# A down projection cut into 512 and 128 columns, its leftovers gathered in one PSUM bank, and every step of the kernel in a new order

## Chip, cores and metric

The kernel runs on one core of a Trainium2 chip. The metric is device time in microseconds (us), lower is better; a run is compared with runs of the other kernel on the same chip. One execution of each kernel is also profiled, and its trace is what this document reads.

## What is computed

Two branches work on the same layer-normed input and are added to it. The input A_q has S = 2048 rows and D = 640 columns; the gated unit has an inner width of F = 1728. All operands are bf16.

```python
x  = A_q
xn = layernorm(x)                                    # over the 640 columns, no gain
# branch A: a convolution over the 2048 rows, channel by channel
k_shift = sum over t of k[s-t] * shift_k[:, t]       # 4 taps
kv = k_shift * v
y  = causal convolution of kv with ssm_k (length 2048, by FFT of length 4096) + kv * ssm_D
A  = xn * y
# branch B: a gated unit
h  = sigmoid(xn @ w_gate) * (xn @ w_up)              # 2048 x 1728
B  = h @ w_down                                      # 2048 x 640
return x + A + B
```

The input `B_x` is not used.

## The kernel before

**Layout.** Row s of the input sits on partition s // 16, in block s % 16, so that a tile of 128 partitions by 16 blocks by 640 columns (`x`, and `xn` for its normed copy) holds everything. The sum builds up in `x`: each branch adds its part there, and the stores read it.

**Branch B** runs in four row groups t of four blocks each. For a group, `xn` is transposed into `xnT` (by TensorE for t = 0, by DMA transposes, `xn_turn`, for the others). Then for each of 13 chunks fc of 128 inner columns, `gate_mm` and `up_mm` (line 291) each make five matmuls of 128x512 into a PSUM tile. ScalarE (ACT) takes the sigmoid (`gate_ev`, line 300), and VectorE (DVE) multiplies it with the up product into `hT` (`up_ev`, line 306). The last 64 inner columns of both go through one product (`both_mm`, line 312; `both_ev`, line 318; `both_mul`, line 321). The down projection follows: for each block bb of the group, 14 matmuls over fc with a 128x128 block of `hT` as the stationary operand and `wd` as the moving one. Before the change it does this once for columns 0 to 319 and once for columns 320 to 639, except for the very last block, which is cut at 512. Each half is issued as two steps of seven matmuls (`down_mm`, line 335), and DVE adds the PSUM result onto `x` (`down_ev`, line 340).

**Branch A** runs in five chunks c of 128 channels, as an FFT convolution in two stages each way:

- `kv_op` (DVE, lines 368 to 377, 16 per chunk) makes kv; `h_turn` (DVE, line 354) transposes the kernel's taps.
- `st1_mm` (lines 393 and 395, 8 per chunk) is the first stage; `st1_ev` copies its PSUM out into tiles `t1`, of which there are two; `wr1` writes each filled tile to DRAM.
- `rd2` reads it back in another layout into tiles `t2`, of which there are two; `st2_mm` (line 427, 4 groups per chunk, numbered s = 0 to 19) is the second stage; `st2_ev` copies it into one of three slots of `xz` (slot s mod 3).
- `prod` multiplies the spectra on DVE: part 0 is a shuffle (line 440), part 1 a multiply (line 442).
- `inv1_mm` (line 456, two per chunk, numbered y = 0 to 9, each on two slots) is the first inverse stage; `inv1_ev` copies out; `wr2` writes to DRAM; `rdb` reads back into `bi`.
- `inv2_mm` (line 495, 4 per chunk) ends the transform; `inv2_q` (line 500) multiplies with `xn` and `inv2_x` (line 505) adds onto `x`.

The PSUM copies of `st1_ev`, `st2_ev` and `inv1_ev` go to ACT (line 254) or to DVE (line 257). PSUM is two pools: `psC`, two tiles of two banks, for branch A's stages (`st2_mm` and `inv1_mm` fill both tiles at once), and `psG`, four tiles of one bank, for all products, down parts and `inv2_mm`.

**Order.** The two branches share all engines. Nothing is scheduled by a planner at build time: steps are appended to chains, one letter a kind (`g` products and down parts, `a` st1_mm, `b` st2_mm, `c` inv1_mm, `d` inv2_mm, `k` kv_op, `u` DVE's steps of branch B, `m` the first loads, `o` the stores, and so on), and a string `ORDER` of one letter a step says in which order they are issued. A capital F, J or I in it is a copy that goes to DVE instead of ACT. `TURNS` reorders the loads and stores within their chains. Each engine then runs its own steps in that order and waits by semaphores. SyncE (SP) issues nearly all DMAs, in the same order; a wait there holds up every later DMA.

Of the kernel before, what the change touches and what calls it, by code (L numbers as in the profile page):

```python
# [11 lines left out]
F32 = mybir.dt.float32  # L12
U16 = mybir.dt.uint16
ACT = mybir.ActivationFunctionType
ALU = mybir.AluOpType

S = 2048
DM = 640
FF = 1728
P = 128  # L20
NB = S // P
NC = DM // P
NFC = 14
# [42 lines left out]
def kernel(  # L66
# [14 lines left out]
    nc = tc.nc  # L81
# [19 lines left out]
    psG = ctx.enter_context(tc.tile_pool(name="psG", bufs=4, space=bass.MemoryType.PSUM))  # L101
# [14 lines left out]
    x = res.tile([P, NB, DM], BF16, name="x")  # L116
# [4 lines left out]
    wd = res.tile([P, NFC, DM], BF16, name="wd")  # L121
    hT = res.tile([P, NFC, 512], BF16, name="hT")
# [199 lines left out]

    pds = {}

    def cols(t, bb, half):
        m = 4 * P if (t, bb) == (3, 3) else DM // 2
        return slice(m, DM) if half else slice(0, m)

    def down_mm(t, bb, half, part):
        es = cols(t, bb, half)  # L330
        if part == 0:
            pds[bb, half] = psG.tile([P, es.stop - es.start], F32, name="pd", tag="g")
        pd = pds[bb, half]
        for fc in range(7 * part, 7 * part + 7):
            nc.tensor.matmul(pd[:, :], lhsT=hT[:, fc, bb * P:(bb + 1) * P], rhs=wd[:, fc, es],  # L335
                             start=(fc == 0), stop=(fc == NFC - 1))

    def down_ev(t, bb, half):
        es = cols(t, bb, half)
        nc.vector.tensor_tensor(x[:, 4 * t + bb, es], pds[bb, half][:, :], x[:, 4 * t + bb, es], ALU.add)  # L340

    def store(b0, b1, lo, hi):
        (nc.scalar if b1 == NB and hi == DM else sync).dma_start(outr[:, b0:b1, lo:hi], x[:, b0:b1, lo:hi])
# [218 lines left out]
    def step(k, fn, *args):  # L562
        chains[k].append((fn, args))

    for t in range(4):
        for fc in range(0 if t else 2, 13):
            step("g", gate_mm, t, fc)
            step("s", gate_ev, t, fc)
            step("g", up_mm, t, fc)
            step("u", up_ev, t, fc)  # L570
        step("g", both_mm, t)
        step("s", both_ev, t)
        step("u", both_mul, t)
        firsts = [(0, 0, 0), (0, 1, 0), (0, 0, 1), (0, 1, 1)]
        for bb, e, part in firsts + [(k // 2, k % 2, n) for k in range(2, 8) for n in range(2)]:
            step("g", down_mm, t, bb, e, part)
            if part:
                step("u", down_ev, t, bb, e)

    def hs(c):  # L580
        return [(load_h, c)]
# [77 lines left out]
        for i in range(4):  # L659
            step("e", xn_turn, g, i)  # L660

    for b in range(0, 12, 2):
        step("o", store, b, b + 2, 0, 4 * P)
    for b in (0, 4, 8):
        step("o", store, b, b + 4, 4 * P, DM)
    for b in range(12, NB - 1):
        step("o", store, b, b + 1, 0, DM)
    step("o", store, NB - 1, NB, 0, 4 * P)
    step("o", store, NB - 1, NB, 4 * P, DM)

    ORDER = """
    mgmLggmmmssugmLuggsmZgmusmmgggmgmuLkHHLgsuksmkggsgmmmuusPlllmmggguklTkkkskkmugsgkumkgsgkmugggsumgKgn
    ekktDauAgakgguIgggLHkeauaggekAuugmDLLkwkeImuguTaaAkkmAgggkHuLwsaaPAgAgggkkkkakuKamkkkwsuggsghwkkAAsK
    aatAugVAuwkkggsHHkarasgukgAAasuggaDwkAAggKTKVsbkkuskkkwBlkggkFKaaAVugkskkpggrAktuusbgkwFBsguhpmuwaAa
    AHDgglsllaanpkkVwuAgsAggreakugpIwagkLkkekgAuuckkTkggCCaAggbBBggarwKkkkukkAKggtHeuubFrBegLuugpbFgBgaa
    kukkpkAAsggVWgkawakskApuugghHaAwDLrrwgspsIaAKugguLVcJCsggpubFpBkggWsbuggpsBuBaAgsakAPnggkspppuucCCgg
    sgrbrkHkglRskkwWBBruugdpbrkgspuBBlgsqdqwcCJqgugsRbBFWggbBBeeuggdkapqlrruqquaAAggldpwqaaAAqegpgagappg
    gIApcuggRJCuuuwebFBwggbuWBppgdquBpgdrrcJsCggqqRbWuFBsppprggsbBguBgsrducqqqdqggRCCbrppBggFubsgguppdBB
    ssqpqcWCdpgrugqqCsqbBFRguugbBBggdssppcgpqdugpqrqCCWusbFBppgWgsguugRcJsguCgsuggggqdduuqqqgguRddqqqgqq
    ggWRRgguuoddogoooqoqqudqdoggoqqoqqooouogguo  # L680
    """
    TURNS = {"m": [18, 21, 0, 5, 1, 10, 2, 7, 4, 14, 9, 6, 15, 12, 13, 11, 8, 17, 16, 20, 23, 22, 25, 24, 26, 19, 3],
        "o": [2, 0, 5, 3, 1, 4, 7, 6, 8, 9, 11, 10, 12, 13]}
    left = {k: iter([v[i] for i in TURNS.get(k, range(len(v)))]) for k, v in chains.items()}
    for k in "".join(ORDER.split()):
        fn, args = next(left[{"F": "B", "J": "C", "I": "A", "Y": "E"}.get(k, k)])
# [32 lines left out]
```

## Time and profile before

| | |
|---|---|
| median of three runs | 235.99 us (235.92 to 236.65) |
| the profiled execution's own time | 236.99 us |
| its span, first to last instruction | 234.9 us |
| TensorE (PE) busy | 227.9 us, 97% of the span, 2281 matmuls |
| VectorE (DVE) busy | 203.0 us, 86% |
| ScalarE (ACT) busy | 133.7 us, 57% |
| DMA | 56.07 MB, mean 239 GB/s |
| TensorE clock granted | 1.000 throughout |

In the profile's rows a line reads: start and duration in us (timeline), or line, engine, operation, output and inputs, shape and count, then busy time and mean duration of one (groups). "PEld" is the weight load that goes before a matmul and overlaps the one ahead of it. Matmuls are pipelined: a row's duration is from the entry of a matmul to the end of its result, and the next one enters earlier than that. So the time that a matmul takes from the engine is the distance from its start to the next start. An entry in square brackets is the idle time ahead of a row and what ended it. The row "DMA to landing" counts from the issue of a DMA to its last packet.

### The profile page before, as it was taken

Reading aid. Unit: us, or ns where it says so; the run is one execution under the profiler, and the core shown is the slowest. Engines: PE = TensorE matmul, PEld = TensorE weight load, DVE = VectorE, ACT = ScalarE, POOL = GpSimd, SP = SyncE. Lnnn points to the kernel's source line nnn. Section 1 sums busy time; section 2 is a strip of 40 time slices with the busy share of each in tenths; the row PEclk is TensorE's granted clock in tenths of the full one; section 3 lists DMA queues with packets and bytes.
Section 4 is the critical chain, followed back from the end, with each engine's and each line's share of the span. In section 5 each row is a group of like instructions: output and inputs, shape, how many; then the busy total and the mean of one; then the engine's idle time right before and its main releaser. Section 6 shows DMA issues by size and latency. Waiting matters only on the chain.

```text
span 234.9 us, 5606 instructions
## 1 busy us (share of the span) xinstructions
PE 227.9 (97%) x2281; PEld 121.9 (52%) x2281; DVE 203.0 (86%) x332; ACT 133.7 (57%) x193; POOL 13.1 (6%) x27
## 2 busy tenths in 40 slices
PE   7999999999999999999999999999899989999994
PEld 2854445665444444666444435476554444447772
DVE  4634899878989999999999999996999999995864
ACT  2477432279766587667687768563466656851000
POOL 5201300101100000000012000000000000000000
PEclk9999999999999999999999999999999999999999
DMA  6997999899998998999997998969999678583485
GB/s 174 325 264 158 293 316 252 168 267 209 314 301 204 257 318 275 213 252 180 290 308 180 305 288 192 307 125 279 317 243 265 184 180 226 139 247 104 140 309 178
DMA packets 97760, 56.07 MB, mean 239 GB/s; under 512 B 55943, under 2 KB 91975, under 8 KB 97607
## 3 DMA queue, kind: packets, MB, share of 16 engines
q1 hardware_dynamic: 97158, 55.35, 90.7%
q10 hardware_dynamic: 576, 0.36, 0.8%
q8 instruction: 18, 0.29, 0.6%
q14 instruction: 8, 0.06, 0.1%
HBM read 35.39 MB, written 18.35 MB: 229 GB/s over the span
## 4 chain that ended last, share of the span: by engine, by line
PE 42%; DVE 9%; DMA 5%; SPq 3%; issue 2%; ACT 1%; DVEq 0%
PE pu L291 11%; PE pd L335 11%; PE pg L291 10%; PE psb L495 3%; DMA d<-t 3%; DMA t<-d 2%; PE ps L427 2%; DVE hT L306 2%; PE psa L456 2%; SPq L271 2%; DVE xz L442 2%; DVE xz L440 1%; PE pg L312 1%; PE ps L395 1%; PE ps L393 1%
## 5 line engine op out<-in xcount | busy, mean ns | idle before, releaser
L291 PEld LDWEIGHTS <-w 128*128 128x128 bf16 x500 | 47.0, 98 | 58.4 <-issue 4.6
L335 PE MATMUL pd<-wd,hT 128*128 128x320 bf16 (+2 forms) x448 | 65.5, 299 | 0.0
L291 PE MATMUL pg<-xnT,w 128*128 128x512 bf16 x250 | 62.1, 379 | 0.3 <-ACT xn L223 0.3
L291 PE MATMUL pu<-xnT,w 128*128 128x512 bf16 x250 | 62.3, 380 | 0.0
L335 PEld LDWEIGHTS <-hT 128*128 128x128 bf16 x448 | 42.3, 98 | 21.3 <-issue 2.0
L254 ACT CAST t<-ps 128x1024 bf16<-128x1024 f32 x35 | 34.4, 1013 | 17.1 <-PE ps L395 11.5
L300 ACT ACTIVATE sig<-pg 128x512 bf16<-128x512 f32 x52 | 30.8, 600 | 23.1 <-PE pg L291 18.5
L306 DVE TENSOR_TENSOR hT<-sig,pu 128x512 bf16<-128x512 bf16 x52 | 34.5, 680 | 10.5 <-PE pu L291 5.7
L254 ACT CAST xz<-ps 128x1024 bf16<-128x1024 f32 x29 | 28.4, 1014 | 13.3 <-PE ps L427 13.2
L442 DVE TENSOR_TENSOR xz<-xz 128x2048 bf16<-128x2048 bf16 x20 | 24.4, 1220 | 0.3
L374 DVE TENSOR_TENSOR acc<-acc,tmp 128x1024 bf16<-128x1024 bf16 x30 | 20.7, 690 | 0.5
L372 DVE TENSOR_TENSOR tmp<-kx,sc 128x1024 bf16<-128x1024 bf16 x30 | 20.6, 686 | 0.4
L340 DVE TENSOR_TENSOR x<-pd,x 128x320 bf16<-128x320 f32 (+2 forms) x32 | 15.1, 484 | 5.0 <-PE pd L335 4.6
L500 DVE TENSOR_TENSOR yx<-psb,xn 128x512 bf16<-128x512 f32 x20 | 13.8, 690 | 2.4 <-PE psb L495 1.3
L395 PE MATMUL ps<-kvh,S1t 128*128 128x512 bf16 x40 | 15.5, 388 | 0.0
L393 PE MATMUL ps<-kvh,S1t 128*128 128x512 bf16 x40 | 15.1, 379 | 0.0
L254 ACT CAST ao<-psa 128x1024 bf16<-128x1024 f32 x12 | 11.8, 1014 | 5.5 <-PE psa L456 5.4
L440 DVE STREAM_SHUFFLE xz<-xz 128x512 f32<-128x512 f32 x20 | 14.5, 724 | 0.0
L257 DVE CAST xz<-ps 128x1024 bf16<-128x1024 f32 x11 | 13.4, 1219 | 0.3 <-PE ps L427 0.2
L495 PEld LDWEIGHTS <-TBt 128*128 128x128 bf16 x160 | 10.1, 98 | 2.9 <-issue 0.8
L223 ACT ACTIVATE xn<-x 128x640 bf16<-128x640 bf16 x12 | 8.8, 735 | 4.7 <-DMA x<-in_A_q_dram 4.7
L354 DVE STREAM_TRANSPOSE kvh<-hn 128x512 f32<-128x512 f32 x10 | 10.8, 1093 | 0.2 <-DMA hn<-in_A_ssm_k_dram 0.2
(54 smaller groups left out, 158.6 us busy)
## 6 DMA issues: line engine op xcount, KB each, us to landing
d<-t SPq DMA_DIRECT2D x20, 512.0 KB, 5.7
t<-d SPq DMA_DIRECT2D x20, 512.0 KB, 6.0
bi<-d SPq DMA_DIRECT2D x8, 512.0 KB, 5.2
d<-ao SPq DMA_DIRECT2D x6, 512.0 KB, 4.1
kx<-in_A_k_dram SPq DMA_DIRECT2D x10, 256.0 KB, 6.0
hn<-in_A_ssm_k_dram SPq DMA_DIRECT2D x20, 128.0 KB, 5.2
kvh<-in_A_v_dram SPq DMA_DIRECT2D x10, 256.0 KB, 6.2
x<-in_A_q_dram SPq DMA_DIRECT2D x3, 640.0 KB, 4.8
```

Of the source, the lines that this page charges most:

```text
L254: nc.scalar.copy(out=out, in_=in_)
L291: nc.tensor.matmul(pg[:, :], lhsT=w[:, c, u * UP + fc * P:u * UP + (fc + 1) * P], rhs=xnT[:, :, c, :], start=(c == 0), stop=(c == NC - 1))
L300: nc.scalar.activation(sig[fc][:, :], pgs[0, fc][:, :], ACT.Sigmoid)
L306: nc.vector.tensor_tensor(hT[:, fc, :], sig[fc][:, :], pgs[1, fc][:, :], ALU.mult)
L335: nc.tensor.matmul(pd[:, :], lhsT=hT[:, fc, bb * P:(bb + 1) * P], rhs=wd[:, fc, es], start=(fc == 0), stop=(fc == NFC - 1))
L372: nc.vector.tensor_tensor(d["tmp"][:, :, :], kx[:, lo + 3 - m:hi + 3 - m, :], sb(m), ALU.mult)
L374: nc.vector.tensor_tensor(d["acc"][:, :, :], d["acc"][:, :, :], d["tmp"][:, :, :], ALU.add)
L393: nc.tensor.matmul(ps[:, 0, :, :], lhsT=S1[:, h, :], rhs=cin[c]["kvh"][:, 0, 4 * n4:4 * n4 + 4, :], start=True, stop=True)
L395: nc.tensor.matmul(ps[:, 1, :, :], lhsT=S1[:, h, :], rhs=hp[:, 2 * n4:2 * n4 + 2, :, :], start=True, stop=True)
L440: nc.vector.stream_shuffle(z[:, 2, :, :].bitcast(F32), z[:, 1, :, :].bitcast(F32), swap)
L442: nc.vector.tensor_tensor(z[:, 1:3, :, :], z[:, 0:1, :, :].to_broadcast((P, 2, 8, P)), z[:, 1:3, :, :], ALU.mult)
L495: nc.tensor.matmul(ps[:, i, :], lhsT=TB[:, h, 4 * m + i, :], rhs=bi[:, h, 4 * (m % 2) + i, :], start=(h == 0), stop=(h == 1))
```

## The change

Four things change together.

- **Down projection.** `down_mm` now makes the first 512 columns of every block (14 matmuls of 128x512 instead of 128x320, again in two steps of seven), and `down_ev` adds them. A new step `rest_mm` makes the last 128 columns of one block, 14 matmuls of 128x128, into a quarter of a PSUM bank that four blocks share; one `rest_ev` then adds all four quarters onto `x`. In the last group the fourth block's rest has a bank and an add of its own.
- **Steps per group.** The chain `g` has 12 down steps in a group instead of 16, and `u` has 5 adds (6 in the last group) instead of 8.
- **Stores.** Blocks 12 and 13 leave together and block 14 alone, first 512 columns each; the last 128 columns of blocks 12 to 14 leave together. Before, blocks 12, 13 and 14 each left whole. There are 14 stores as before.
- **Order.** `ORDER` and `TURNS` are new throughout. Of the 100 PSUM copies of branch A, 77 instead of 79 now go to ACT and 23 instead of 21 to DVE (st1: 7 instead of 5; st2: 10 instead of 11; inv1: 6 instead of 5).

```diff
-    def cols(t, bb, half):
-        m = 4 * P if (t, bb) == (3, 3) else DM // 2
-        return slice(m, DM) if half else slice(0, m)
-
-    def down_mm(t, bb, half, part):
-        es = cols(t, bb, half)
+    def down_mm(t, bb, part):
         if part == 0:
-            pds[bb, half] = psG.tile([P, es.stop - es.start], F32, name="pd", tag="g")
-        pd = pds[bb, half]
+            pds[bb] = psG.tile([P, 4 * P], F32, name="pd", tag="g")
         for fc in range(7 * part, 7 * part + 7):
-            nc.tensor.matmul(pd[:, :], lhsT=hT[:, fc, bb * P:(bb + 1) * P], rhs=wd[:, fc, es],
+            nc.tensor.matmul(pds[bb][:, :], lhsT=hT[:, fc, bb * P:(bb + 1) * P], rhs=wd[:, fc, 0:4 * P],
                              start=(fc == 0), stop=(fc == NFC - 1))
 
-    def down_ev(t, bb, half):
-        es = cols(t, bb, half)
-        nc.vector.tensor_tensor(x[:, 4 * t + bb, es], pds[bb, half][:, :], x[:, 4 * t + bb, es], ALU.add)
+    def down_ev(t, bb):
+        b = 4 * t + bb
+        nc.vector.tensor_tensor(x[:, b, 0:4 * P], pds[bb][:, :], x[:, b, 0:4 * P], ALU.add)
+
+    def rest_mm(t, bb, b0):
+        if bb == b0:
+            pds[t, b0] = psG.tile([P, 4, P], F32, name="pr", tag="g")
+        for fc in range(NFC):
+            nc.tensor.matmul(pds[t, b0][:, bb, :], lhsT=hT[:, fc, bb * P:(bb + 1) * P], rhs=wd[:, fc, 4 * P:DM],
+                             start=(fc == 0), stop=(fc == NFC - 1))
+
+    def rest_ev(t, b0, b1):
+        xs = x[:, 4 * t + b0:4 * t + b1, 4 * P:DM]
+        nc.vector.tensor_tensor(xs, pds[t, b0][:, b0:b1, :], xs, ALU.add)
...
-        firsts = [(0, 0, 0), (0, 1, 0), (0, 0, 1), (0, 1, 1)]
-        for bb, e, part in firsts + [(k // 2, k % 2, n) for k in range(2, 8) for n in range(2)]:
-            step("g", down_mm, t, bb, e, part)
+        for bb, part in ((0, 0), (1, 0), (0, 1), (1, 1), (2, 0), (2, 1)):
+            step("g", down_mm, t, bb, part)
             if part:
-                step("u", down_ev, t, bb, e)
+                step("u", down_ev, t, bb)
+        last = [(0, 3), (3, 4)] if t == 3 else [(0, 4)]
+        for b0, b1 in last:
+            if b1 == 4:
+                step("g", down_mm, t, 3, 0)
+                step("g", down_mm, t, 3, 1)
+                step("u", down_ev, t, 3)
+            for bb in range(b0, b1):
+                step("g", rest_mm, t, bb, b0)
+            step("u", rest_ev, t, b0, b1)
...
-    for b in range(0, 12, 2):
+    for b in range(0, 14, 2):
         step("o", store, b, b + 2, 0, 4 * P)
-    for b in (0, 4, 8):
-        step("o", store, b, b + 4, 4 * P, DM)
-    for b in range(12, NB - 1):
-        step("o", store, b, b + 1, 0, DM)
+    step("o", store, 14, 15, 0, 4 * P)
+    for b in (0, 4, 8, 12):
+        step("o", store, b, min(b + 4, 15), 4 * P, DM)
...
-    TURNS = {"m": [18, 21, 0, 5, 1, 10, 2, 7, 4, 14, 9, 6, 15, 12, 13, 11, 8, 17, 16, 20, 23, 22, 25, 24, 26, 19, 3],
-        "o": [2, 0, 5, 3, 1, 4, 7, 6, 8, 9, 11, 10, 12, 13]}
+    TURNS = {"m": [6, 0, 1, 4, 21, 5, 13, 2, 7, 15, 9, 10, 12, 14, 8, 17, 18, 11, 16, 20, 22, 23, 19, 25, 24, 26, 3],
+        "o": [5, 0, 6, 3, 1, 7, 4, 2, 8, 10, 9, 11, 12, 13]}
```

(`ORDER` is replaced as a whole and not shown.)

More of the change, by code (lines that the diff above doesn't have):

```diff
@@ L671 @@
     ORDER = """
[L672 to L680, printed above, removed]
-    """
-    TURNS = {"m": [18, 21, 0, 5, 1, 10, 2, 7, 4, 14, 9, 6, 15, 12, 13, 11, 8, 17, 16, 20, 23, 22, 25, 24, 26, 19, 3],
-        "o": [2, 0, 5, 3, 1, 4, 7, 6, 8, 9, 11, 10, 12, 13]}
+    mmmmmggsmgggsuuggsgmLgLumssZLLPmguggumggmsgmkmkkuslgsTkmkukuggsummgsmmHHmmggugDkksumlggsgllugkkkkkkk
+    kHHaamAnggAtkaaImueeggkuuwAagaeeAAkkLggkgmuDgamwLgsAaAwkkkkmgLgsKKaAgakukkkkkgusuggAsTkugagtwaLkkgsI
+    AuuggkkkakhHHgwnsauKKsgVAAPlgsauklTwIkLkkrgaggruwVAVsDlbgklBuggBsawuagAAgbgkkssgkkKkFuuatkBhaIgkgAwm
+    paakLsprswkgupukKKKHAAwggLpaaAkugAgceuggCCbkkkHDkgkkLgBFkkeuuaapggAeAVpTgeurbFPBpgstgrbkuBggwBkaaskk
+    gguIgAsgkksuKVhHrkwawAWaAkggDaAparApukgnkpkssgcCVJuuggbFwBWggssubBBkwppgskgaaIuuggrAcgpJgrpsuCbsFRWk
+    BgsugupbBprgsBllgugscCdlrpdkukkkwegeqqClHbBBRggbBgWrFqaeIagAdaaquqqupdpgAAppwaaAuggrAqqucCeJRwgggbpw
+    WBFpgugbrrdqpqgsdRgBBpcuggJqCWbgsusFBgsubggBppdBdpqqppcrsCCrguugsbFgguBsRbpggrrBpBdcqqqsWdqCggpCuqpq
+    bFBRpruggsbWpBBuqsggcpJCdqusgupbdWBBggsqppgsugRcCJuqqggRdqqsWgdRugdqqqdquRogggqogguuqooooddqqqqogddo
+    qqgggoqoquuuoooo
+    """
+    TURNS = {"m": [6, 0, 1, 4, 21, 5, 13, 2, 7, 15, 9, 10, 12, 14, 8, 17, 18, 11, 16, 20, 22, 23, 19, 25, 24, 26, 3],
+        "o": [5, 0, 6, 3, 1, 7, 4, 2, 8, 10, 9, 11, 12, 13]}
     left = {k: iter([v[i] for i in TURNS.get(k, range(len(v)))]) for k, v in chains.items()}
```

## The prediction

> **What bounds the kernel now.** I read the page's busy times and its chain first, then the waits, then the timeline of TensorE at each place where it stood still.
>
> ```profile
> PE 227.9 (97%) x2281; PEld 121.9 (52%) x2281; DVE 203.0 (86%) x332; ACT 133.7 (57%) x193; POOL 13.1 (6%) x27
> PE 42%; DVE 9%; DMA 5%; SPq 3%; issue 2%; ACT 1%; DVEq 0%
> ```
>
> PE is busy for 227.9 of 234.9 us. An edit can save time in two ways only: less work on PE, or fewer gaps in it. So the question is what a matmul takes from PE, and where PE stood still. The first is read from starts in the last microseconds, where PE runs unhindered:
>
> ```profile
> 219.99 4.92 PE L335 MATMUL pd<-wd,hT 128*128 128x320 bf16 x35
> 224.74 1.06 PE L495 MATMUL psb<-bi,TBt 128*128 128x128 bf16 x16
> 227.48 3.97 PE L335 MATMUL pd<-wd,hT 128*128 128x512 bf16 x28
> ...
> L335 PE MATMUL pd<-wd,hT 128*128 128x320 bf16 x420 | 61.5, 299 | 0.0
> L335 PE MATMUL pd<-wd,hT 128*128 128x128 bf16 x14 | 0.9, 219 | 0.0
> L335 PEld LDWEIGHTS <-hT 128*128 128x128 bf16 x448 | 42.3, 98 | 21.3 <-issue 2.0
> ```
>
> Thirty-five matmuls of 320 columns take 4.92 us, the last of them 299 ns to its end: (4.92 - 0.30) / 34 = 136 ns from start to start. Sixteen of 128 columns: (1.06 - 0.22) / 15 = 56 ns. The third timeline row is the last block, already cut into 14 of 512 and 14 of 128 columns: 3.97 - 0.22 - 13 x 0.056 = 3.02, or 216 ns for each of the wide ones.
>
> The places where PE waited longest after its start-up (columns: start, duration, what, idle ahead and what ended it):
>
> ```profile
> 20.33 1.24 PE L291 MATMUL pu<-xnT,w 128*128 128x512 bf16 x5
> 21.86 1.25 PE L291 MATMUL pg<-xnT,w 128*128 128x512 bf16 x5 [0.29 <-ACT xn L223]
> ...
> 101.86 3.62 SPq L271 DMA_TRANSPOSE xnT<-xn  x1
> 108.79 2.08 PE L335 MATMUL pd<-wd,hT 128*128 128x320 bf16 x14
> 110.96 0.44 PE L427 MATMUL ps<-t,FWt 32*32 32x256 bf16 x32
> ...
> 157.59 0.82 SPq L407 DMA_DIRECT2D d<-t  x1
> 162.85 2.06 PE L335 MATMUL pd<-wd,hT 128*128 128x320 bf16 x14
> 164.41 1.22 DVE L257 CAST t<-ps 128x1024 bf16<-128x1024 f32 x1 [2.25 <-DMA d<-t]
> 165.68 0.65 PE L456 MATMUL psa<-xz,SMt 32*32 32x512 bf16 x32 [0.77 <-DVE t L257]
> ...
> 191.13 0.61 PE L495 MATMUL psb<-bi,TBt 128*128 128x128 bf16 x8
> 191.89 0.71 DVE L440 STREAM_SHUFFLE xz<-xz 128x512 f32<-128x512 f32 x1
> 192.66 0.65 PE L456 MATMUL psa<-xz,SMt 32*32 32x512 bf16 x32 [0.92 <-DVE xz L440]
> ```
>
> The bracket leaves out the pipeline's overlap, so I take starts. (A) Five matmuls from 20.33 take 5 x 0.216 = 1.08 and the next starts at 21.86: 0.45 us lost. (B) 14 x 0.136 from 108.79 ends at 110.69, the next starts at 110.96: 0.27, the read `rd2(4)` that it needs having stood behind a 3.62 us transpose on SP. (C) From 162.85 the same way: 0.93; `inv1_mm(4)` needs the PSUM tiles that two copies of `st1_ev` hold, and these need the buffer that the write issued at 157.59 empties. (D) 191.13 + 8 x 0.056 to 192.66: 1.08; `inv1_mm(7)` waits for the shuffle of group 16, which the list has ahead of it, and DVE was late. Together 2.73 us.
>
> **Part by part.** *PE's work.* Every pair of 320s (2 x 136 = 272 ns) becomes a 512 and a 128 (216 + 56 = 272 ns). Fifteen blocks change, 14 pairs each; rounding leaves at most 1 ns for each of 210 pairs, 0.2 us either way. I take 0. Matmuls and weight loads stay 2281. Here a rule of the Trainium skill speaks against the change (TensorE: Matmul & The Clock Gate, section Back-to-back issue gap): in a stream where every matmul has its own weight load, it gives about 81 ns for 128 columns and calls 56 too low. By it the sum would have 210 x (81 - 56) = 5.3 us more. The 16 matmuls at 56 ns above each had a weight load, so the trace disagrees.
>
> *DVE's work.* Rows for its steps, and for how much of it was idle between the `both_mul` of one row group and the next:
>
> ```profile
> L340 DVE TENSOR_TENSOR x<-pd,x 128x320 bf16<-128x320 f32 x30 | 14.1, 483 | 4.8 <-PE pd L335 4.6
> L340 DVE TENSOR_TENSOR x<-pd,x 128x512 bf16<-128x512 f32 x1 | 0.7, 691 | 0.1
> L340 DVE TENSOR_TENSOR x<-pd,x 128x128 bf16<-128x128 f32 x1 | 0.3, 292 | 0.1
> L306 DVE TENSOR_TENSOR hT<-sig,pu 128x512 bf16<-128x512 bf16 x52 | 34.5, 680 | 10.5 <-PE pu L291 5.7
> L442 DVE TENSOR_TENSOR xz<-xz 128x2048 bf16<-128x2048 bf16 x20 | 24.4, 1220 | 0.3
> L257 DVE CAST xz<-ps 128x1024 bf16<-128x1024 f32 x11 | 13.4, 1219 | 0.3 <-PE ps L427 0.2
> L440 DVE STREAM_SHUFFLE xz<-xz 128x512 f32<-128x512 f32 x20 | 14.5, 724 | 0.0
> L500 DVE TENSOR_TENSOR yx<-psb,xn 128x512 bf16<-128x512 f32 x20 | 13.8, 690 | 2.4 <-PE psb L495 1.3
> L505 DVE TENSOR_TENSOR x<-x,yx 128x512 bf16<-128x512 bf16 x20 | 8.4, 421 | 0.4
> ...
> 40.37:95.91 55.54, 55.54 (x360) 28.85 (x358) 51.26 (x80) 38.07 (x58) 3.21 (x5) 1.00 1.00 255
> 95.91:152.45 56.54, 56.45 (x699) 28.24 (x696) 55.67 (x84) 41.02 (x57) 2.46 (x3) 1.00 0.99 252
> 152.45:214.01 61.56, 59.87 (x849) 31.76 (x822) 56.27 (x90) 35.80 (x43) 0.00 (x0) 1.00 0.83 217
> ```
>
> (In the last three rows the fourth number is DVE's busy time.) The 32 adds cost 14.1 + 0.7 + 0.3 = 15.1 us. Afterwards there are 16 + 3 of 512 elements, 19 x 0.691 = 13.1, one of 384 that I put at 0.56 between its neighbours, one of 128: 14.0. That saves 1.1 us; two copies moved over from ACT cost 2 x 1.22 = 2.4. DVE gets 1.3 us more in all. Counting the steps between one `both_mul` and the next in the new order, by the same durations, its stretches come to 53.7, 53.8 and 61.3 us. PE's steps between the `both_mm` before them make 54.2, 55.9 and 62.3. In before's middle stretch DVE was 98% busy and PE lost only (B), so that alone does not stall PE; the loops inside do.
>
> So I looked, in the new order, for every place where PE waits for DVE or ACT, and compared the work in between on both sides. The tightest: `inv1_mm(9)` needs the products of group 19, and DVE starts on that string when `inv1_mm(7)` has read its slots. In it stand four multiplies, four shuffles, two copies, five `up_ev`, two `inv2_q`, three `inv2_x`: 4 x 1.22 + 4 x 0.724 + 2 x 1.219 + 5 x 0.68 + 2 x 0.69 + 3 x 0.421 = 16.3. Back to back these overlap: the durations in the middle stretch add up to 60.6 against 55.67 busy, 0.92 of it. So 15.0, and some 0.4 for the two hand-overs, 15.4. PE meanwhile has eleven products (11 x 1.08), three each of `inv2_mm` (8 x 0.056) and `st2_mm` (0.44), one `inv1_mm` (0.65): 15.2. A stall of 0.2, with 2% of 15 either way: 0.3. A second string, 43 DVE instructions from `st2_ev(1, 0)` to `st2_ev(5, 0)`, comes out 27.0 against 26.9: 0.2. I take 0.5 for both, 0 to 1.4.
>
> *(A)* goes: that weight chunk (gate, columns 768 to 1023) had 2,368 KB of loads ahead of it on SP; now it has 960 KB. Behind it ACT has four statistics steps (the first two rows below are their halves) and three sigmoids before PE needs the PSUM tile of the third: 4 x (0.735 + 0.828) + 3 x 0.6 = 8.1 us, 9.6 with the accumulator reads if nothing hides them, against 9.0 of PE's steps. I take 0, up to 0.6.
>
> ```profile
> L223 ACT ACTIVATE xn<-x 128x640 bf16<-128x640 bf16 x12 | 8.8, 735 | 4.7 <-DMA x<-in_A_q_dram 4.7
> L224 ACT ACTIVATE xn<-x,lnq 128x640 bf16<-128x640 bf16 x12 | 9.9, 828 | 0.4
> L254 ACT CAST t<-ps 128x1024 bf16<-128x1024 f32 x35 | 34.4, 1013 | 17.1 <-PE ps L395 11.5
> L300 ACT ACTIVATE sig<-pg 128x512 bf16<-128x512 f32 x52 | 30.8, 600 | 23.1 <-PE pg L291 18.5
> ```
>
> *(B)* goes: `rd2(4)` now has 8.2 us of PE's work between the release of its buffer and its use; it had 6.6. *(D)* goes: the list now has `inv1_mm(7)` ahead of that shuffle. *(C)* stays. The same write now waits for one copy on each engine, of which DVE's 1.22 is the longer: 1.35 us after `st1_mm(4, 3)` with the hand-over. How long it takes to land is in these rows (smallest, median, largest):
>
> ```profile
> DMA to landing us min/median/max: 4.0/5.7/7.0
> DMA to landing us min/median/max: 4.2/6.0/7.2
> ```
>
> The first is `wr1`, the second `rd2`. After the landing both copies are now on ACT, one after the other: 2 x 1.01 where the two engines side by side took 1.22. In (C) it took 164.41 - 157.59 = 6.8, by the start of DVE's copy. With 1.35 + 5.7 to 6.8 + 2.0 = 9.1 to 10.2 against 8.7 us of PE's steps: 0.4 to 1.5. I take 0.8. *(E, new)* `rd2(19)` has 7.0 us between release and use, where before it had 8.5; it needs 6.0 at the median and 0.4 for the hand-overs, up to 7.6: 0.2, 0 to 0.6.
>
> *What SP is moved past.* The four transposes of each group, the k, v and taps loads and `rdb` stand elsewhere in SP's queue. By their places I find each read landing 0.5 to 2 us ahead of its use: cover that one long issue eats, a rival below. The shared bank adds a wait: `rest_ev` waits for four `rest_mm`, but in three groups DVE reaches it after PE is done. The bank is held 4 x 0.79 = 3.1 us, while the other three turn.
>
> *The tail.*
>
> ```profile
> 230.71 1.07 DVE L340 TENSOR_TENSOR x<-pd,x 128x512 bf16<-128x512 f32 x2
> ```
>
> Now DVE's last add ends at 231.78, 0.33 after PE (227.48 + 3.97). In the new order, from the start of `inv2_mm(4, 0)`, PE has 6.4 us left and DVE 0.45 + 0.3 for the first result, four `inv2_q` and four `inv2_x` (4.4) and adds of 384, 512 and 128 elements (1.5): 6.7, and up to 0.5 for the gaps between dependent steps. So DVE ends 0.2 to 0.7 after PE's result; I take 0.5, which makes the tail 0.2 longer, -0.1 to 0.6. The split stores carry the same bytes and are issued before that.
>
> *The sum.* Span 234.9 - 2.73 (A to D) + 0.8 (C) + 0.5 (strings) + 0.2 (E) + 0.2 (tail) = 233.9. Small waits that I cannot place will come on top, as PE's gaps that are not in my list did before; I add 0.2: 234.1, 0.8 less. The profiled execution took 236.99, 1.0 above the median of the runs shown; the difference is made against the median: 235.99 - 0.8 = 235.2. About 0.3% (0.7 us) is what a measurement of this kernel can tell from no change, so the forecast lies just beyond it.
>
> **Rivals.** *SP's long issues (slower).* A transpose holds SP for very different times:
>
> ```profile
> L271 SPq DMA_TRANSPOSE xnT<-xn x12: 1225/1448/4557, 44.3 to 162.7; - x12
> ```
>
> Two stand back to back ahead of `rdb(0, 1)` and one ahead of the write of (C). One that takes 4.6 instead of 1.4 us puts what follows 3.2 later. `inv2_mm(0, 2)`, whose read has 1.7 us of cover, then starts 1.5 late; the write, for which SP is free some 1.7 early, makes (C) 1.5 longer; `rd2(4)`, behind the second group's four and with 1.9 of cover, costs 1.3. All together -0.8 + 4.3 = +3.5: 239.5. With one or two of them, which I take for this rival, half of the 4.3: +1.3, 237.3. It decides from 0.8 us of such stalls on. For it: the share of DMA time is 1.00 and 0.99 in the rows from 40 to 152 us. Against: the median is 1.45, and before the change such issues cost PE only (B).
>
> *DVE becomes the bound.* With 0.94 instead of 0.92 for the overlap, the two strings lose 0.9 and 0.4 rather than 0.5 together, and the two copies more that DVE now makes for `st1_ev` can be held by a landing as ACT's are now: 0.5 to 1. That cancels the gain: 236.0, 235.4 to 236.7. For it: 61.3 of 62.3 us in the last stretch. Against: DVE has 3.0 to 5.1 us of PE's steps between a `both_mm` and the half that needs `both_mul`, before 1.9 to 2.8.
>
> *The weight load shows at 128 columns (slower).* A load lasts 98 ns and a matmul of 128 columns enters every 56. If the load were not hidden, each of the 210 new narrow matmuls would take up to 98: +8.8 us at the most, 244.0. The sixteen and the fourteen at 56 ns, each with a load of its own, speak against it. By the 81 ns of the Trainium skill's TensorE page it would be 240.5.
>
> *The new shape does nothing* is part of the forecast itself: all of the gain comes from the order.
>
> **How the numbers follow.** Forecast 0.43 (faster); DVE as the bound 0.25 (within 0.3%); SP's issues 0.29 (slower); the 128 columns 0.03 (slower). So faster 0.43, same 0.25, slower 0.32. The range: with (C) at 0.4, the strings and (E) at nothing and the tail at -0.1, the sum is 2.73 - 0.3 = 2.4 below, 233.6; nearly all must go well for that, so I cut at 234.0. Upwards it takes in DVE's case and SP's to 0.4 beyond its middle: 237.7. Left out are the rest of SP's case (0.1), the 128 columns and the very low end, under 0.2.
>
> **What would show it.** Right: PE's matmuls of 512 and 128 columns at 216 and 56 ns from start to start; no gap in the first 25 us; none before `inv1_mm(7)`; about 0.8 us before `inv1_mm(4)`, ended by the copies of `st1_ev`; DVE's busy time near 204. Wrong: gaps over 1 us in front of `inv2_mm(0, 2)` or `st2_mm(4)`, ended by DMAs (SP's case), gaps that end with DVE's copies or `up_ev` all through 100 to 150 us (DVE's), or 128-column matmuls at 80 ns.

## The result, and the profile after

| | before | after |
|---|---|---|
| median of 11 executions each, same chip | 236.13 us (235.60 to 236.76) | 235.00 us (234.75 to 235.94) |
| ratio | | 0.9951 (95% interval 0.9937 to 0.9965), 1.2 us less |
| profiled execution: time / span | 236.99 / 234.9 us | 235.94 / 234.2 us |

The forecast was 235.2 us and faster. The sum behind it was right in sign and nearly in size, but not in all of its terms; that it came within 0.2 us is in part luck, as the account below shows.

The page of the changed kernel: busy time, share of the span and count of instructions of each engine, then the chain of waits by engine.

```profile
PE 227.0 (97%) x2270; PEld 112.8 (48%) x2281; DVE 204.1 (87%) x323; ACT 131.5 (56%) x191; POOL 12.7 (5%) x27
PE 79%; DVE 12%; DMA 4%; issue 2%; SPq 1%; ACT 1%; DVEq 0%
```

The chain's share of PE, 79% where it was 42%, is no measure of the gain: before's shares add up to only 62%, and b_gate_early, below, shows PE at 87% with 1.39 us of stalls left. (Eleven matmul records are missing; the weight loads, 2281, are complete.) What PE waited for does show it (us in total, times, longest):

```profile
PE pg L282 <- DMA w<-in_B_w_gate_dram: 1.3, 1, 1.3
PE idle L528 <- DVE hT L128: 1.2, 1, 1.2
PE pd L329 <- issue: 0.2, 1, 0.2
```

The first two are of the start-up, the third of 0.2 us is a missing record. (A), (B), (C) and (D) are gone. This view leaves out the pipeline's overlap, so the small stalls show by starts alone. The timeline of TensorE in the changed kernel:

```profile
113.25 1.24 PE L291 MATMUL pu<-xnT,w 128*128 128x512 bf16 x5
114.43 0.82 PE L432 MATMUL ps<-t,FWt 32*32 32x256 bf16 x32
115.18 1.25 PE L291 MATMUL pg<-xnT,w 128*128 128x512 bf16 x5
...
193.22 0.61 PE L500 MATMUL psb<-bi,TBt 128*128 128x128 bf16 x8
193.76 0.65 PE L461 MATMUL psa<-xz,SMt 32*32 32x512 bf16 x32
...
218.83 3.62 PE L329 MATMUL pd<-wd,hT 128*128 128x512 bf16 x16
222.29 1.73 PE L340 MATMUL pr<-wd,hT 128*128 128x128 bf16 x28
```

Three things are to be seen. The last two rows give (3.62 - 0.38) / 15 = 216 ns and (1.73 - 0.22) / 27 = 56 ns from start to start: the new shape runs as forecast. The pair at 193 us is where stall (D) stood: 193.22 + 8 x 0.056 = 193.67, and `inv1_mm(7)` starts at 193.76. The 0.09 between is no wait: there are 30 changes from 128x128 to 32x32 tiles in each kernel, and at every one where nothing is waited for it stands, 0.093 long. And in the first rows `st2_mm(4)` lasts 0.82 instead of the usual 0.44: the longest stall that is left, 0.31 us by starts.

With stalls counted by starts, less that 0.093, each profile falls into three parts: when the first product of 512 columns starts, how long PE stood from there on, and the rest. The rest, the start of the last matmul less the first two, is between 215.8 and 216.3 us in all profiles of this case, 216.0 in both kernels: PE's work did not change at all.

| kernel | first product at | stalls | last matmul at | span | median, ratio to before (interval) |
|---|---|---|---|---|---|
| before | 12.78 | 2.44: A 0.45, B 0.16, C 0.84, D 0.99 | 231.23 | 234.9 | |
| after | 13.75 | 0.49 | 230.24 | 234.2 | 235.00, 0.9951 |
| a_again | 12.67 | 0.50 | 229.17 | 233.2 | 235.08, 0.9950 (0.9930 to 0.9970) |
| b_shape | 12.65 | 2.29: C 0.32, D 0.99, new 0.98 | 230.84 | 234.8 | 237.06, 1.0024 (1.0005 to 1.0043) |
| b_inv1_first | 12.98 | 1.35: A 0.69, C 0.19, rest 0.47 | 230.46 | 234.6 | 235.91, 0.9986 (0.9967 to 1.0006) |
| b_gate_early | 12.59 | 1.39: C 0.32, D 0.99, 0.08 | 230.01 | 234.3 | 236.66, 1.0007 (0.9990 to 1.0023) |
| b_mend | 12.82 | 2.41: reads 1.97, 0.44 | 231.37 | 235.3 | 236.13, 0.9982 (0.9962 to 1.0002) |
| a_read_first | 13.15 | 0.77: C 0.27, 0.50 | 230.11 | 233.9 | 235.17, 0.9954 (0.9934 to 0.9974) |
| a_old_first | 12.65 | 0.50 | 229.16 | 233.1 | 234.85, 0.9928 (0.9910 to 0.9946) |
| a_string | 12.70 | 0.31 | 228.92 | 232.9 | 234.75, 0.9917 (0.9902 to 0.9933) |
| a_dve_more | 12.67 | 1.29 | 230.23 | 234.1 | 236.07, 0.9983 (0.9968 to 0.9999) |
| a_both | 12.54 | 0.30 | 228.79 | 232.6 | 234.90, 0.9942 (0.9921 to 0.9963) |
| a_turn_late | 12.66 | 0.47 | 229.14 | 233.0 | 234.80, one execution |

(Kernels with b_ are edits of before, those with a_ of the changed one. Medians are of different sessions; the ratio is to before in the same one.)

So between the two profiles the stalls fell by 1.95 us, the start came 0.98 later, and from the last matmul to the end of the span it took 3.92 instead of 3.67: 234.9 - 1.95 + 0.98 + 0.25 = 234.2. The late start is taken up with a_again, below; the last part is 3.7 to 4.3 us in all profiles, without a pattern.

### The profile page after: what moved, and what is told of

Read it like the earlier page. It is cut to its first block, busy times and chain, and to the rows that moved or that the text cites. A ratio compares the mean times of both kernels' runs of the same rounds, so it can differ in the third digit from the quotient of the medians.

```text
span 234.2 us, 5584 instructions
## 1 busy us (share of the span) xinstructions
PE 227.0 (97%) x2270; PEld 112.8 (48%) x2281; DVE 204.1 (87%) x323; ACT 131.5 (56%) x191; POOL 12.7 (5%) x27
## 4 chain that ended last, share of the span: by engine, by line
PE 79%; DVE 12%; DMA 4%; issue 2%; SPq 1%; ACT 1%; DVEq 0%
PE pg L291 22%; PE pu L291 22%; PE pd L329 14%; PE psb L500 3%; PE pr L340 3%; PE ps L400 3%; PE ps L398 3%; DMA w<-in_B_w_up_dram 3%; PE ps L432 3%; PE psa L461 2%; DVE tmp L377 2%; PE pg L312 1%; DVE acc L379 1%; DVE yx L505 1%; DMA SMt<-tabSM 1%
## 5 line engine op out<-in xcount | busy, mean ns | idle before, releaser
L329 PE MATMUL pd<-wd,hT 128*128 128x512 bf16 x213 | 50.4, 379 | 0.7 <-issue 0.2
L254 ACT CAST t<-ps 128x1024 bf16<-128x1024 f32 x33 | 32.3, 1013 | 21.9 <-PE ps L400 21.9
L254 ACT CAST xz<-ps 128x1024 bf16<-128x1024 f32 x30 | 29.5, 1015 | 14.3 <-PE ps L432 14.3
L329 PEld LDWEIGHTS <-hT 128*128 128x128 bf16 x224 | 21.3, 98 | 25.1 <-issue 0.9
L254 ACT CAST ao<-psa 128x1024 bf16<-128x1024 f32 x11 | 10.8, 1014 | 8.3 <-PE psa L461 8.2
L340 PE MATMUL pr<-wd,hT 128*128 128x128 bf16 x224 | 13.8, 219 | 0.0
L340 PEld LDWEIGHTS <-hT 128*128 128x128 bf16 x224 | 13.0, 98 | 1.8 <-issue 0.6
L334 DVE TENSOR_TENSOR x<-pd,x 128x512 bf16<-128x512 f32 x16 | 10.7, 684 | 2.1 <-PE pd L329 2.0
L257 DVE CAST xz<-ps 128x1024 bf16<-128x1024 f32 x10 | 12.1, 1215 | 0.4 <-PE ps L432 0.4
```

The source lines that it names most:

```text
L254: nc.scalar.copy(out=out, in_=in_)
L329: nc.tensor.matmul(pds[bb][:, :], lhsT=hT[:, fc, bb * P:(bb + 1) * P], rhs=wd[:, fc, 0:4 * P], start=(fc == 0), stop=(fc == NFC - 1))
L340: nc.tensor.matmul(pds[t, b0][:, bb, :], lhsT=hT[:, fc, bb * P:(bb + 1) * P], rhs=wd[:, fc, 4 * P:DM], start=(fc == 0), stop=(fc == NFC - 1))
```

## The experiments

**b_shape: the new columns in before's order.** Each block's four steps keep their letters and nearly their PE time:

```diff
-        for fc in range(7 * part, 7 * part + 7):
-            nc.tensor.matmul(pd[:, :], lhsT=hT[...], rhs=wd[:, fc, es], ...)      # es: one half of 320
+        wide, rest = [(0, fc) for fc in range(NFC)], [(1, fc) for fc in range(NFC)]   # 0: 512 columns, 1: 128
+        todo = ([rest, wide[0:5], wide[5:9], wide[9:]] if bb else
+                [wide[0:5], wide[5:7] + rest[0:7], rest[7:] + wide[7:10], wide[10:]])[k]
```

> The kernel before with its own order, letter for letter, and only the down projection cut into 512 and 128 columns (each block's four steps keep nearly the PE time that they had; the 128-column part has a bank of its own). Theory, as in the prediction: the shape does nothing by itself, PE's starts stay 216 and 56 ns apart, all four stalls of before stay, and the time is that of before within 0.3%. Rival 1, the weight load shows at 128 columns: 25 to 42 ns for each of 210 narrow matmuls, 5 to 9 us slower. Rival 2, the shape is what brought the gain: 1.1 us faster than before.

Measured: 1.0024, 0.6 us slower (0.1 to 1.0). No gain comes from the shape, and no price of the narrow matmuls either: PE's work is 215.9 us. What it cost in this order is waits (waits of PE):

```profile
PE psa L463 <- DVE xz L447: 0.9, 1, 0.9
...
PE pd L341 <- DVE x L347: 0.3, 1, 0.3
```

(D) stands as before; new is a wait for a PSUM bank that DVE's adds had not yet emptied (0.42 us by starts), with 0.56 in three more gaps, one of them a weight load that waits for `both_mul`. I put these down to how I fitted the steps to the old letters, not to the columns; no run shows which. Rivals 1 and 2 fell. The Trainium skill (TensorE: Matmul & The Clock Gate, section Back-to-back issue gap) would have had 81 ns for each narrow matmul; at 56 ns in both kernels the traces disagree. The 320-column halves in the new order were not tried, since their eight PSUM tiles a group do not fit its letters: that the new order would gain the same with the old columns is argued from PE's equal work, not shown.

**b_inv1_first: stall (D) alone taken away.**

```diff
-  ... q p q c W C ...      # prod(16, 0), inv2_q, inv1_mm(7)
+  ... q q c p W C ...      # inv2_q, inv1_mm(7), prod(16, 0)
```

> The kernel before with one letter of its order moved: the shuffle of group 16 stands behind inv1_mm(7) instead of ahead of it, so that stall (D) has no cause left. Theory 1, stalls add up: the wait of 0.99 us (1.08 less the 0.093 that any change from 128x128 to 32x32 tiles costs) is gone and the time falls by 1.0. Theory 2, DVE is the bound behind that place: its last multiply ahead of inv1_mm(9) ends 0.57 us before that step in before, and DVE stands idle for no more than 0.3 us in between, so a PE that comes 1.0 earlier stops for 0.2 to 0.5 us at inv1_mm(8) or inv1_mm(9), and the time falls by only 0.5 to 0.7.

Measured: 0.9986, 0.3 us less, and the interval (0.8 less to 0.1 more) takes in no change. TensorE and DVE in its timeline:

```profile
191.42 0.65 PE L456 MATMUL psa<-xz,SMt 32*32 32x512 bf16 x32
...
197.35 0.28 PE L427 MATMUL ps<-t,FWt 32*32 32x256 bf16 x2
197.79 0.43 PE L427 MATMUL ps<-t,FWt 32*32 32x256 bf16 x30 [0.15 <-DVE xz L257]
```

```profile
193.18 1.23 DVE L442 TENSOR_TENSOR xz<-xz 128x2048 bf16<-128x2048 bf16 x1
...
196.52 1.22 DVE L257 CAST xz<-ps 128x1024 bf16<-128x1024 f32 x1
```

0.97 of the 0.99 us is gone at its place, and 0.36 comes back six microseconds later: `st2_mm` finds its second PSUM tile held by a copy that DVE, busy nearly without a pause, has not finished. Theory 2 had the size in the profile (0.97 less 0.36 and 0.03 leaves 0.58) and the cause, but looked for it one step later, at `inv1_mm`; there only the 0.03 was lost.

**b_gate_early: stall (A) alone taken away.**

```diff
-    "m": [18, 21, 0, 5, 1, 10, 2, 7, 4, 14, ...
+    "m": [18, 21, 0, 4, 1, 10, 2, 7, 5, 14, ...
```

> The kernel before with two of its first loads exchanged on SP: the gate weights of columns 768 to 1023 take the place of the up weights of the same columns, which PE needs one product later. Theory: stall (A) of 0.45 us at 21.2 us goes and nothing comes for it: the time falls by 0.4 to 0.5. Rival, the loads are late as a whole (they land in the order of their issue, 1.1 us apart): the up weights are then as late as the gate weights were, less one product of 1.08 us, and since PE also comes 0.45 earlier the stall moves there with 0 to 0.3 us: 0.2 to 0.5 less. The first product should begin where it begins in before, at 7.25 us, if its start is set by what is loaded first; if it varies by a microsecond from one profiled execution to the next, this run and the other two on the kernel before will show it.

Measured: 1.0007 (0.9990 to 1.0023), no gain. In its profile nothing is lost in the first 25 us, and (C) and (D) stand:

```profile
PE psa L456 <- DVE xz L440: 0.9, 1, 0.9
PE psa L456 <- DVE t L257: 0.3, 1, 0.3
```

Across the profiles (A) varies: with before's loads it is 0.45, in b_shape nothing, in b_inv1_first 0.69. It is a matter of one execution to the next, and so is (C): 0.84, 0.32, 0.19 and 0.32 us. (B), 0.16 in before, is absent in all four others in before's order: there the same long transpose stood ahead, 3.6 to 3.7 us, but the read landed 0.2 to 0.7 us before PE came to it. Only (D) is the same each time: 0.99, 0.99, 0.99. One profile of before had overstated (B) and (C). For (A) that is not shown: three profiles make 0.38 on average, and the interval of this run leaves at most 0.24 for its mending; why it is not more stays open.

**a_read_first: why (C) is gone.**

```diff
-  ... A A p p w a a A u g g r A ...      # wr1(4, 1), then rd2(12)
+  ... A A p p r w a a A u g g A ...
```

> The changed kernel with one read, rd2(12), issued on SP ahead of the write wr1(4, 1) of place (C) instead of right behind it. In the changed kernel that write landed 3.4 us after its issue (6.6 in before, where two reads of 512 KB and a transpose were issued within 3 us ahead of it), and place (C) is not a stall any more. Theory 1, the landing is set by the bytes that are queued ahead: with 512 KB more ahead the write lands some 2 us later, 5 to 6 us after its issue, the two copies of st1_ev end about 0.7 to 1.2 us later, and a stall of 0 to 0.5 us comes back at inv1_mm(4): time 0 to 0.5 more. Theory 2, the 3.4 was chance or the place in the order does not matter: landing between 3.4 and 4.5 us, no stall, same time.

In the changed kernel (SP):

```profile
159.76 0.34 SPq L412 DMA_DIRECT2D d<-t  x1
```

The same write, with its KB and the us from issue to landing, then ACT and PE:

```profile
d<-t SPq DMA_DIRECT2D x1, 512.0 KB, 3.4
```

```profile
164.00 1.93 ACT L254 CAST t<-ps 128x1024 bf16<-128x1024 f32 x2 [0.96 <-PE ps L400]
```

```profile
167.31 0.65 PE L461 MATMUL psa<-xz,SMt 32*32 32x512 bf16 x32
```

The two copies wait for PE only: the write, issued at 159.76, is through at 163.2, before they start at 164.0, and they end 1.4 us ahead of `inv1_mm(4)`. With the read ahead of the write (SP, the write's landing, ACT, PE):

```profile
157.64 0.55 SPq L422 DMA_DIRECT2D t<-d  x1
159.18 0.42 SPq L412 DMA_DIRECT2D d<-t  x1
```

```profile
d<-t SPq DMA_DIRECT2D x1, 512.0 KB, 5.9
```

```profile
165.20 1.93 ACT L254 CAST t<-ps 128x1024 bf16<-128x1024 f32 x2 [2.74 <-DMA d<-t]
```

```profile
166.73 1.10 PE L461 MATMUL psa<-xz,SMt 32*32 32x512 bf16 x32
```

The write now takes 5.9 us, the copies wait for it, and `inv1_mm(4)` is stretched by 0.27 us. Theory 1 holds, and not in this pair of profiles alone. In the five in which one or two 512 KB reads are issued within 2.3 us ahead of this write (before, b_shape, b_inv1_first, b_gate_early, a_read_first) it takes 5.9 to 6.6 us to land; in the other eight, where the last read ahead is more than 6 us back, 3.3 to 4.2. The time (0.9954) cannot tell 0.27 us; the verdict rests on these rows.

**a_dve_more: is DVE's string as tight as forecast?**

```diff
-  ... p B B u q ...      # st2_ev(18, 1) on ACT
+  ... p B F u q ...      # st2_ev(18, 1) on DVE
```

> The changed kernel with one more PSUM copy on DVE: the second half of st2_ev(18) goes to DVE instead of ACT, in the string between inv1_mm(7) and inv1_mm(9). In the changed kernel DVE's last multiply for inv1_mm(9) ended 0.21 us ahead of that step, and a step that waits for DVE starts 0.06 us after it at the soonest, so 0.15 us is spare. Theory 1, the string's balance is as close as the prediction had it (15.4 against 15.2): 1.22 - 0.15 = 1.0 to 1.1 us of stall at inv1_mm(9) and 0.9 to 1.1 us more in all. Theory 2, DVE was far from bounding and its steps only sit waiting: 0 to 0.3 us.

Measured: 0.9983, against 0.9951 and 0.9950 for the changed kernel: 0.8 us more. Stalls went from 0.50 to 1.29. DVE and PE:

```profile
200.56 1.22 DVE L257 CAST xz<-ps 128x1024 bf16<-128x1024 f32 x1
...
203.24 1.22 DVE L257 CAST ao<-psa 128x1024 bf16<-128x1024 f32 x1
```

```profile
201.83 0.65 PE L461 MATMUL psa<-xz,SMt 32*32 32x512 bf16 x30 [0.19 <-DVE xz L257]
...
204.51 0.44 PE L432 MATMUL ps<-t,FWt 32*32 32x256 bf16 x30 [0.19 <-DVE ao L257]
```

The size is a little under theory 1's 0.9 to 1.1 and far from theory 2's; the place is neither's. PE stops for 0.40 us each at the two steps whose second PSUM tile a DVE copy still holds, and then meets `inv1_mm(9)` without a wait. As in b_inv1_first a late DVE shows first in the copies, since PSUM has only two tiles for these stages.

**a_string: the stalls that are left.**

```diff
-  ... g e u r b F P B p g s t g r b k u B g g w B k a ...      # u: rest_ev(1), up_ev(2, 0)
+  ... g e r b F u P B p g s t g r b k B g g w B k u a ...      # F: st2_ev(3, 0), last k: kv_op(3, 15)
```

> The changed kernel with two letters of its order moved on DVE: rest_ev(1) behind the copy of st2_ev(3, 0) instead of ahead of it, and up_ev(2, 0) behind kv_op(3, 15). In the changed kernel PE stopped 0.31 us inside st2_mm(4) at 114.4 us, where its second PSUM tile was still held by that copy, and 0.10 us at 117.1 us for kv_op(3, 15). Theory 1, both are matters of order inside a string that DVE has time for: both stalls go, 0.4 us less, which is the least that can be told from nothing. Theory 2, DVE is the bound of that string as a whole, as the prediction's second string had it (27.0 against 26.9 us): one stall goes and 0.2 to 0.4 us comes back at the next step that waits for DVE.

Measured: 0.9917 (0.9902 to 0.9933), the lowest ratio of all. DVE in its timeline, and what PE waited for:

```profile
111.89 1.22 DVE L257 CAST xz<-ps 128x1024 bf16<-128x1024 f32 x1
113.03 0.68 DVE L345 TENSOR_TENSOR x<-pr,x 128x512 bf16<-128x512 f32 x1
```

```profile
113.37 0.44 PE L432 MATMUL ps<-t,FWt 32*32 32x256 bf16 x32
```

```profile
PE pg L291 <- DVE hT L306: 0.2, 1, 0.2
```

In the changed kernel the add of the four blocks' 128 columns (L345) stood ahead of the copy, and the copy ended at 114.75. Turned round, `st2_mm(4)` is back at 0.44 us, and the wait for `kv_op(3, 15)` is gone too. But at 130 us PE now waits 0.23 for `up_ev`: as theory 2 had it, about half of the gain is given back where DVE is next late, though both stalls went and not one. 0.2 us is left in the profile.

**b_mend: before, mended at three places.** The edits of b_gate_early and b_inv1_first, and the reads `rd2(11)` and `rd2(12)` behind the write of (C):

```diff
-  ... a p q l r r u q q u a A A g g l d p w q ...
+  ... a p q l u q q u a A A g g l d p w r r q ...
```

> The kernel before with three small edits of its order and nothing of the new shape: the gate weights of columns 768 to 1023 exchanged with the up weights on SP (A), the two reads rd2(11) and rd2(12) issued behind the write wr1(4, 1) instead of ahead of it (C), and the shuffle of group 16 behind inv1_mm(7) (D). Theory 1, the changed kernel's gain is the mending of these places, and can be had without the shape and without the rest of the new order: the stalls fall from 2.4 to 0.4 to 0.8 us in the profile, the write lands 4 to 5 us after its issue, and the time is 1.0 to 1.6 us below before, as good as the changed kernel's or better. Theory 2, what is mended at one place comes back at the next (DVE behind D, the reads behind C): stalls of 1.2 us or more are left and the time is 0.3 to 0.8 below before.

Measured: 0.9982 (0.9962 to 1.0002). Its profiled execution was the longest of its twelve (237.38), so its stalls are above the usual; the places are what counts. SP and PE:

```profile
157.65 0.34 SPq L407 DMA_DIRECT2D d<-t  x1
...
159.65 4.10 SPq L271 DMA_TRANSPOSE xnT<-xn  x1
...
170.88 3.56 SPq L417 DMA_DIRECT2D t<-d  x2
```

```profile
177.44 0.44 PE L427 MATMUL ps<-t,FWt 32*32 32x256 bf16 x32 [1.27 <-DMA t<-d]
```

(A), (C) and (D) are gone: the write landed 3.8 us after its issue. In their place PE waits 1.34 us for a read that SP issued only at 170.88, 1.4 later than in before; from the transpose that held SP for 4.10 on, SP issued one DMA after the other without a pause. This is the prediction's first rival, found in the old order instead of the new one. Another 0.63 us at 85.7, behind a read that took 9.0 us to land, stands ahead of the edits for (C) and (D); with the same order there b_gate_early had 6.7 and no stall. The gain of the changed kernel was not had by mending these three places in this way; theory 1 fell.

**a_old_first, a_again, a_both: was the late start the kernel's?** a_old_first changes the list of first loads, a_again nothing, and a_both joins a_old_first and a_string.

```diff
-    "m": [6, 0, 1, 4, 21, 5, 13, 2, 7, 15, 9, 10, 12, 14, 8, 17, 18, 11, 16, ...
+    "m": [18, 21, 0, 1, 4, 5, 6, 2, 7, 15, 9, 10, 13, 12, 14, 8, 17, 11, 16, ...
```

> The changed kernel with only its list of first loads in another order: S1t (64 KB) and the x of group 1 (640 KB) go first, as in before, then the weight chunks. In the four profiles of kernels with before's first loads, PE's first product of 512 columns began at 12.6, 12.6, 12.8 and 13.0 us; in the two with the changed kernel's at 13.2 and 13.8. Theory 1, the loads that stand right behind the first four weight chunks set when those chunks land: the first product is back at 12.6 to 13.0, PE meets no stall in the first 25 us, and the time falls by 0.4 to 0.8 against the changed kernel (ratio to before some 0.992 to 0.993). Theory 2, the start varies by chance: 12.6 to 13.8 here too, time as the changed kernel's (0.995). Rival to both: with 704 KB ahead of the weights again a stall of the kind of (A) comes back, 0.3 to 0.7 us.

> The changed kernel itself, unaltered, beside the two versions that were faster than before by more than it. Of nine profiles, the first product of 512 columns began at 12.6 to 13.0 us in seven and at 13.2 and 13.8 in two, both with the changed kernel's first loads; a_string, which has the same first loads, began at 12.7. Theory 1, the late start of the changed kernel's first profile was chance: 12.6 to 13.2 here, stalls of 0.5 us again at the same three places, span near 233.2, time 234.8 to 235.1. Theory 2, it belongs to the kernel: 13.2 to 13.8 and a span of 234.

> The changed kernel with the edits of a_string (rest_ev and up_ev behind, on DVE) and of a_old_first (S1t and x of group 1 ahead of the weights). If the two differences to the changed kernel are real and have nothing to do with each other: stalls of 0.1 to 0.3 us, start at 12.6 to 12.8, 0.4 to 0.7 below the changed kernel. If the start was chance, only a_string's 0.2 to 0.4 are left.

The same row in the first profile of the changed kernel and in that of a_again:

```profile
8.13 0.73 PE L282 MATMUL pg<-xnT,w 128*128 128x128 bf16 x10 [1.34 <-DMA w<-in_B_w_gate_dram]
```

```profile
7.05 0.73 PE L282 MATMUL pg<-xnT,w 128*128 128x128 bf16 x10 [0.17 <-DMA w<-in_B_w_gate_dram]
```

The same kernel, one microsecond apart, with stalls of 0.49 and 0.50 us at the same three places. The late start does not belong to the kernel: of six profiles with the changed kernel's first loads, four began at 12.66 to 12.70 us. Whether it is rarer with before's first loads (none of seven profiles began after 12.98) is not shown. (Of the ten profiles up to then, eight and not seven had begun by 13.0.) So the first profile (235.94, the longest of its eleven) was 0.9 above the kernel's own median for that reason; before's (236.99) was 0.9 above its own too, most likely by the stalls that vary. a_old_first, at 234.85, has the changed kernel's stalls and no shown gain from its loads, and a_both keeps only a_string's 0.2: 234.90 beside 235.08 in the same session, 234.42 to 235.14 and 234.92 to 235.38. That difference, 0.1%, is too small for the timing to settle; a_string's ratio in its own session is 0.3% lower than the changed kernel's in two others, so how much it gains stays open.

**a_turn_late: whom SP's long issue hits.**

```diff
-  ... w e g e q q C l H b B B R g g b B g W r F q a e ...      # second e: xn_turn(3, 1), r: rd2(11)
+  ... w e g q q C l H b B B R g g b B g W r e F q a e ...
```

> The changed kernel with one transpose, xn_turn(3, 1), moved on SP behind the read rd2(11). Before's long issues on SP were transposes (4.56 us at 150.0, 3.62 at 101.9), as the prediction's rival had it; in the changed kernel no transpose takes over 1.94 us, but a read, rd2(11), takes 3.30 at 153.2. Theory 1, a long issue belongs to the moment, when much is queued, and falls on whatever SP issues then: rd2(11) now takes 0.4 to 1.5 us and the transpose behind it, or the next DMA, 2.5 to 3.5. Theory 2, it belongs to that read: 3.3 us again, and the transposes stay below 2. By both the time is that of the changed kernel, since the read and the transpose are needed 10 us later.

```profile
151.74 4.68 SPq L422 DMA_DIRECT2D t<-d  x1
156.51 1.48 SPq L271 DMA_TRANSPOSE xnT<-xn  x1
```

Neither number of theory 1 came: the read, not the transpose, took 4.68 us. Beside a_again, whose first product began at the same time (12.67 and 12.66), the read was issued 0.4 earlier and ended 0.5 later (3.78 us, to 155.91, there; to 156.42 here). In all eight profiles in the new order this read takes 3.3 to 4.7 us, which is theory 2 but for its 3.3 (the longest transpose takes 2.07); a queue that happens to be full whenever this read comes would look the same. It stays open.

## Why the prediction was right, and where its steps were not

*PE's work, 0*: right. PE's part without stalls is 216.0 us in both kernels, and the matmuls of 512 and 128 columns stand 216 and 56 ns apart.

*DVE's work, +1.3, 204 in all, stretches of 53.7, 53.8 and 61.3*: right. From one `both_mul` to the next in the changed kernel (fourth number: DVE):

```profile
40.65:97.36 56.71, 56.60 (x363) 27.02 (x363) 53.91 (x81) 40.00 (x65) 2.05 (x4) 1.00 0.92 249
97.36:152.12 54.76, 54.39 (x627) 25.13 (x627) 53.87 (x80) 36.05 (x47) 3.69 (x4) 1.00 0.92 248
152.12:215.47 63.35, 63.19 (x905) 31.31 (x908) 61.18 (x94) 36.72 (x44) 0.00 (x0) 1.00 0.84 226
```

*Stalls A to D, 2.73*: mis-sized. They were 2.44: at (B), (C) and (D) I had counted the 0.093 of the change of tiles as waiting. That price is paid at 30 places afterwards too. The Trainium skill (TensorEngine Tiling (Array Packing), section Tiling Modes) says that a change of tiling mode drains the engine; the trace agrees, with 0.093 us. And (A), (B) and (C) vary, as shown with b_gate_early; that before's median lies 0.9 below the execution that I had fits this. So the going of (A) and (B) cannot be put down to the new order for sure, while (D) was the same each time and went with its one letter. So 1.95 us less of stalls (1.94 against a_again) became 1.2 in the medians.

*(C) stays at 0.8*: wrong, and the largest wrong term. The step that failed is the landing: I took the median of all writes and the 6.8 of before (5.7 to 6.8), though the new order has less queued ahead of this write. It landed in 3.4 us and left 1.4 us of cover; with the read put ahead it took 5.9 and there was a stall of 0.27.

*Strings on DVE, 0.5*: the sum was right (0.41), the shares not. The string to `inv1_mm(9)` cost nothing: from 194.34, where PE goes on from `inv1_mm(7)`, DVE took 15.2 to the end of the last multiply (15.4 in the sum), but PE took 15.4 and not 15.2. I had left out five changes of tiles there (0.46), and had counted `st2_mm` and `inv1_mm` 0.27 too long, by their rows' durations instead of from start to start. So 0.15 us was spare, and one copy more, a_dve_more, cost 0.8. The other string took all: 0.31 inside `st2_mm(4)` and 0.10 for `kv_op(3, 15)`.

*(E) 0.2 and small waits 0.2*: there was nothing at (E), and one small wait of 0.08 ahead of the last block. *Tail 0.2*: DVE ended 0.34 after PE's result, where it had ended 0.33 after it, so this term was 0. The 0.25 more from the last matmul to the end of the span lies behind DVE's last add, and such a difference stands between profiles of one kernel too (3.92 and 4.04).

In stalls the sum had 1.0 us less (the 0.8 of the forecast and the 0.2 of the tail), and the profiles show 1.95 less: (C), (E), the strings and the small waits were together 1.2 too pessimistic, A to D 0.3 too optimistic. In the medians only 1.2 of it came, since before's usual time has fewer stalls than its profile. The errors went both ways, so that 235.2 met 235.0 is luck in part; the mechanism, no change in PE's work and a gain by fewer stalls, was right.

*The rivals.* SP's long issues did not come where I had put them. The transposes in the changed kernel and in b_mend (ns, min/median/max):

```profile
L271 SPq DMA_TRANSPOSE xnT<-xn x12: 1205/1292/1936, 43.6 to 160.6; - x12
```

```profile
L271 SPq DMA_TRANSPOSE xnT<-xn x12: 1227/1742/4102, 42.1 to 166.8; - x12
```

I had taken the long issue for a property of a transpose and moved it with the step. In all five profiles in before's order some transpose takes 3.7 to 4.6 us, in none of the eight in the new order more than 2.6; there a read, `rd2(11)`, issued at 151.7 to 153.2 us, takes 3.3 to 4.7, and PE does not wait for it. DVE as the bound did not happen, but is one copy away: 0.8 us. (In that rival, 0.94 of the added durations makes 0.5 and 0.7 us for the two strings by the sums above it, not 0.9 and 0.4; together that is nearly the same.) The weight load at 128 columns did not show.

## What to carry to other kernels

Measure stalls by starts, and subtract what every such change of instruction costs where nothing waits, or the same 0.1 us is first counted as gain and then missing in the sum of a string. A landing time is not a property of a transfer (3.4 and 5.9 us for the same write): look at what is issued in the few microseconds ahead of it, in the new order. And take two profiles before mending a stall: here the one that was the same in all of them (D) left 0.58 us in the profile and 0.3 in the time when mended alone, since DVE was late right behind it, and one that varied (A) brought nothing that the time shows. (C) was not mended alone.

## What was not expected of the hardware

Two executions of the same kernel differed by 1.08 us in when the first weights had landed (PE's first product of 128 columns at 8.13 and at 7.05 us), with PE's steps after it the same distance behind to 0.05 us. A late DVE stopped PE less at the step that needs DVE's product (0.10 in the changed kernel, 0.03 in b_inv1_first) than at one that needs a PSUM tile which a copy on DVE still holds (0.31 and 0.36, and twice 0.40 in a_dve_more).
